# A first phase in chunks of 512 tokens instead of 384, on a kernel that runs on one TensorE

## The chip, the cores and the metric

The kernel runs on one core of one Trainium2 chip. The metric is the device time of one execution, in microseconds; lower is better. Engine names: PE (TensorE), DVE (VectorE), ACT (ScalarE), POOL (GpSimd), SP (the queue that issues most DMAs).

## The reference, cut to what matters

Linear attention, then a dense two-layer network, then a network of eight experts of which each token goes to one:

```
kv   = einsum('bhsd,bhse->bhde', k, v)            # 8 batches, 8 heads, 576 tokens, 64 wide
out  = einsum('bhsd,bhde->bhse', q, kv)
out  = out / sqrt(mean(out*out) + 1e-6) * g_norm  # per head
x    = out as [4608 tokens, 512]
h    = x @ w_in                                   # 512 -> 2048
y    = (max(h,0) + alpha*min(h,0)) @ w_out        # 2048 -> 512
e    = argmax(y @ w_gate + bias[modality]), p = softmax value of e
res  = p * (max(y @ w1[e], 0) @ w2[e])            # 8 experts, 512 -> 1024 -> 512
```

## The kernel before, in words

Every product of the networks is made of three products of a high part and a low part (hi x hi, hi x lo, lo x hi), all in fp32r.

The first phase takes the tokens in 12 chunks of CT = 384 (three tiles of 128). A chunk has 16 blocks `s`, one for each 128 of the 2048 hidden values. In block `s`, `first(c, s)` does 12 matmuls with the weights standing and the chunk's columns moving (L382, into a PSUM bank 384 wide). DVE then makes `gg` of it in two instructions (L388, L389), ACT rounds it to `ghi` (L393), POOL subtracts to `glo` (L395). `second(c, s - 1)` does nine matmuls (L409): each of ghi x w, ghi x w_low, glo x w for three tiles, 512 columns of the weights moving. So what `first(c, s)` gives is used one block later. At the chunk's end the next chunk's input is taken (`take_x`, L369, L370), and the last `second` is split over the boundary.

Between the matmuls each engine works, in program order, through what was put into the same blocks:

- `dots(c - 1)`: the eight routing logits of each tile of the chunk before, one DVE multiply-and-sum over 512 each (L426). DOTS says which of the 24 are done in which block; in the last chunk LAST_DOTS. Then `choose`, `weigh`, `count` (two small matmuls, L480, L481), `place`, `scatter` (indirect DMAs on POOL to the expert's rows in `xb`).
- For the next chunk: `kv_mm` (k times v of a batch that begins in it, 40 matmuls, L232), `attend` (q times kv, 64 matmuls for each tile, L249), `attended` (ACT copies and squares, L259, L260), `squares` (DVE sums, L295), `rsqrt`, `scale_x`, `turn_x`.
- Pieces of the expert weights: 128 times ACT rounds (L215) and POOL subtracts (L219) 512 columns, and SP stores them (`wsp`).

In chunk 0 the first network's weights come in and are cut into parts as they are used (`cut`), and before it there is a head: batch 0's kv, attention, norm and transposes for chunk 0, with idle transposes (`warm`, L858) on PE in between.

The second phase does 41 tiles of sorted rows, 24 matmuls a layer (`layer1`, `layer2`, L685). The first four tiles belong to one expert, chosen before the last chunk is routed; while they run, the last chunk's logits, places, `padding`, `table` and row loads are done. The order written there is the order on every engine's queue.

Of the kernel before, what the change touches and what calls it, by code (L numbers as in the profile page):

```python
# [26 lines left out]
CT = 384  # L27
# [16 lines left out]
DOTS = (0, 2, 5, 8, 11, 14, 17, 20, 22, 24)  # L44
LAST_DOTS = (0, 3, 7, 10, 14, 17, 21, 24)
# [3 lines left out]
def fused(ctx: ExitStack, tc, qT, kv, kv0, g2, wmoe, alpha, wgate, bias, modality, w12, out):  # L49
# [16 lines left out]
    kvt = phase1.enter_context(tc.tile_pool(name="kvp", bufs=1)).tile([128, 2, 5, 256], F32, name="kvt")  # L66
# [10 lines left out]
    pad = one.tile([128, ROW], F32, name="pad")  # L77
    yrow = [one.tile([128, ROW], F32, name=f"yrow{i}") for i in range(3)]
# [10 lines left out]
    xs = one.tile([128, 3, D], F32, name="xs")  # L89
# [17 lines left out]
    def other(n=512):  # L107
        return (pools[1] if pools else ps_a).tile([128, n], F32, tag="a", name="a")
# [117 lines left out]
    def kv_mm(b, p):  # L226
# [26 lines left out]
    def attended(c, t):  # L253
        ps = ops_t.pop((c, t))
        x = xs[:, t, :].rearrange("p (a h b) -> p a h b", a=4, h=2)
        sq = junk.rearrange("p (a h b) -> p a h b", a=4, h=2)
        xt_t[c, t] = xs[:, t, :].rearrange("p (a b) -> p a b", b=64)
        for h in range(2):
            A.copy(x[:, :, h, :], ps[h])  # L259
            A.activation(sq[:, :, h, :], ps[h], AF.Square)  # L260

    def kv_pair(p):

        t = kv_t.pop((0, p))
        kvp = ps_y.tile([128, 128], F32, tag="y", name="kvp") if p < 3 else bank(128)
# [9 lines left out]
    def attend_pair(p):  # L275
        for t in range(3):
            PE.matmul(ops[t][:, p, :], q_t[0][:, p, t * 128:(t + 1) * 128], kvbd[0][:, p, :], start=True, stop=True)

    def square_half(t, h):
        if t < 2:  # L280
            sq = (junk, pad)[t][:, h * 256:h * 256 + 256]
        else:
            sq = two.tile([128, CT], F32, tag="gg", name="sq")[:, 0:256]
# [7 lines left out]
    def squares(c, t):  # L291
        sq = junk.rearrange("p (a b) -> p a b", b=64)
        if t == 0:
            ms_t[c] = one.tile([128, 24], F32, tag="ms", name="ms")
        V.tensor_reduce(ms_t[c][:, t * 8:t * 8 + 8], sq, AX.X, ALU.add)  # L295

    def rsqrt(c, others=(), part=None):
# [5 lines left out]
        if c > 1:  # L303
            it, m = spare[:, 96:120].bitcast(I32), spare[:, 120:144]
        else:
            a = other(48) if c else bank(48)
            it, m = a[:, 0:24].bitcast(I32), a[:, 24:48]
        u = one.tile([128, 24], F32, tag="u", name="u")
# [6 lines left out]
        else:  # L315
            half, to = (one.tile([128, 24], F32, name=n) for n in ("half", "root"))
# [7 lines left out]
        if part == 0:  # L324
            sq = lambda: V.tensor_reduce(ms[:, 16:24], junk.rearrange("p (a b) -> p a b", b=64), AX.X, ALU.add)
            fill(list(others) + steps[:4], [sq])
        else:
            fill(steps, others)
# [15 lines left out]
    def scale_first(h):  # L344
        for t in range(3):
            r = ms_t[0][:, t * 8:t * 8 + 8]
            src = ops[t] if t < 2 else last
            to = xs[:, t, :].rearrange("p (h e a i) -> p a h e i", h=2, e=2, a=4)
# [4 lines left out]
    def turn_first(k):  # L353
        ps = ps_y.tile([128, CT], F32, tag="y", name="first") if k < 2 else spare[:, 0:CT] if k == 2 else bank(CT)
        for t in range(3):
            PE.transpose(ps[:, t * 128:(t + 1) * 128], xs[:, t, k * 128:(k + 1) * 128], ident)
        return ps

    def turn_x(c, t):
        x = xs[:, t, :]  # L360
        V.transpose(x, x)

    def take_x(c, k):
        if c:
            of = xs.rearrange("p t (a k j) -> p (t a) k j", a=4, k=4)[:, :, k]
# [7 lines left out]
    def first(c, fb, between=None):  # L373
# [9 lines left out]
        gg = two.tile([128, CT], F32, tag="gg", name="gg")  # L383
# [8 lines left out]
        ghi = two.tile([128, CT], F32R, tag="ghi", name="ghi")  # L392
        A.copy(ghi, gg)  # L393
        glo = two.tile([128, CT], F32R, tag="glo", name="glo")
# [3 lines left out]
    def second(c, fb, parts=(0, 1, 2)):  # L398
        ghi, glo = g_t[c, fb]
        if fb == 0:  # L400
            y_t[c] = [ps_y.tile([128, D], F32, tag="y", name="y") for _ in range(3)]
# [4 lines left out]
        for i in parts:  # L406
            a, w = steps[i]
            for t in range(3):
# [3 lines left out]
    B3 = [128, 3, E]  # L412
    ul = lambda a: a.unsqueeze(2).to_broadcast(B3)

    def y_out(c, t):
        if t == 1:
            lg_t[c] = one.tile([128, 3, E], F32, tag="lg", name="lg")
# [46 lines left out]
    def weigh(c):  # L464
# [3 lines left out]
        sm = one.tile([128, 3], F32, tag="sm", name="sm")  # L468
        V.tensor_reduce(sm, ex, AX.X, ALU.add)
        V.tensor_scalar(sm, sm, 1e-9, None, ALU.add)  # L470
        gate = one.tile([128, 3], F32, tag="gate", name="gate")
        V.reciprocal(gate, sm)
        for t in range(3):
            V.tensor_copy(yb_t[c][t][:, D:D + 1], gate[:, t:t + 1])
            V.tensor_copy(yb_t[c][t][:, D + 1:D + 2].bitcast(I32), tokid[:, c * 3 + t:c * 3 + t + 1])

    def count(c):
        hot, hb, lg = hot_t[c]
        ps = (other(48) if pools else spare[:, 0:48]).rearrange("p (n a b) -> p n a b", n=2, a=3)
# [4 lines left out]
    def place(c):  # L484
        hot, ps, _ = hot_t.pop(c)
        at = one.tile(B3, F32, tag="bt", name="at")
        for t in range(3):
# [3 lines left out]
        mx = one.tile([128, 3], F32, tag="mx", name="mx")  # L491
        V.tensor_reduce(mx, at, AX.X, ALU.add)
        pos = one.tile([128, 3], I32, tag="pos", name="pos")
# [12 lines left out]

    def padding():
# [4 lines left out]
        for e in range(E):  # L512
# [3 lines left out]
            i = SP.dma_start(xb[ds(r, 128)], pad)  # L516
# [22 lines left out]
    def table():  # L539
# [12 lines left out]
        tmp = two.tile([1, CT], F32, tag="gg", name="tmp")  # L552
# [17 lines left out]
        ge = two.tile([1, CT], F32, tag="gg", name="ge")[:, 0:NTAB * E].rearrange("p (a b) -> p a b", b=E)  # L570
# [60 lines left out]
    def load_rows(i):  # L631
# [7 lines left out]
        rows[i] = four(xs[:, i % 3, :])  # L639
# [6 lines left out]
    def load_first():  # L646
        r = SP.value_load(tab_0[0:1, 1:2], min_val=0, max_val=E * BUCKET)
        src = xb[ds(r, 3 * 128)]
        to = xs.rearrange("p t (a c) -> p (t a) c", a=4)
# [3 lines left out]
        for i in range(3):  # L653
            rows[i] = four(xs[:, i, :])
# [91 lines left out]
    def halves(i):  # L746
        if i not in ht:
            ht[i] = (pools[2].tile([128, 2, 512], F32R, tag="kv", name="hth"),
# [83 lines left out]
    with tc.manual_schedule():  # L832
# [28 lines left out]
        ops.extend(four(b) for b in (other(), other(), spare))  # L861
# [292 lines left out]
```

## Time and profile before

| | |
|---|---|
| median of 3 runs | 1342.45 us (1342.27 to 1343.2) |
| the profiled execution | 1342.6 us, span 1341.0 us |
| PE, DVE, POOL, ACT busy | 99%, 74%, 50%, 39% of the span |
| PEld (weight loads, beside PE) | 86% |
| first matmul of chunk 0 / first of the second phase | 20.34 us / 876.53 us |
| PE clock granted | 0.999 of full |

The span is from the first to the last instruction; the time adds what lies around it. "Busy" counts a matmul from its start to its modelled end, and matmuls overlap, so a PE that is busy all the time can still start its matmuls later than it might; the distance between starts tells that.

### The profile page before, as it was taken

How to read it: one execution, taken by the hardware profiler on the slowest of the kernel's cores; microseconds unless marked ns; L12 is line 12 of the kernel's file. 1: busy time of each engine (PE TensorE's matmuls, PEld its weight loads, DVE VectorE, ACT ScalarE, POOL GpSimd, SP SyncE). 2: the span in 40 equal slices, each digit the busy share in tenths (PEclk: the TensorE clock that was granted, in tenths of full speed). 3: DMA queues.
4: the chain of work that ended last, by engine and by line, in shares of the span. 5: the costliest groups of instructions: out<-in, count | busy, mean ns of one | idle time of the engine just before them, and what ended most of it. 6: DMA issues, size and time to landing. Idle time of an engine off the chain costs nothing. (4 is left out here: it accounts for less than half of the span.)

```text
span 1341.0 us, 26648 instructions
## 1 busy us (share of the span) xinstructions
PE 1332.3 (99%) x8864; PEld 1150.0 (86%) x8864; DVE 990.2 (74%) x2216; ACT 526.5 (39%) x1153; POOL 669.0 (50%) x648
## 2 busy tenths in 40 slices
PE   9999999999999999999999999999999999999997
PEld 8889888889888889888888988888888888888886
DVE  5789687878878777878687969576766666666664
ACT  5762323333333332332323331144544444444443
POOL 5867475656655555656474652353333333333321
PEclk9999999999999999999999999999999999999999
DMA  8955565554555564556564440547311271737784
GB/s 321 329 199 199 200 209 202 189 191 142 197 184 195 191 203 149 193 186 213 193 215 152 147 146 1 209 165 264 125 49 49 76 268 48 281 98 302 295 320 186
DMA packets 82325, 250.69 MB, mean 187 GB/s; under 512 B 12877, under 2 KB 32077, under 8 KB 80016
## 3 DMA queue, kind: packets, MB, share of 16 engines
q1 hardware_dynamic: 70432, 220.82, 46.3%
q0 software_dynamic: 11760, 28.14, 6.4%
q8 instruction: 78, 1.28, 0.4%
q14 instruction: 55, 0.45, 0.1%
HBM read 158.69 MB, written 91.54 MB: 187 GB/s over the span
## 5 line engine op out<-in xcount | busy, mean ns | idle before, releaser
L382 PE MATMUL h<-xhi,W 128*128 128x384 f32 x1536 | 427.7, 341 | 0.0
L395 POOL TENSOR_TENSOR glo<-gg,ghi 128x384 fp32r<-128x384 f32 x192 | 234.8, 1223 | 336.1 <-ACT ghi L393 330.4
L409 PE MATMUL y<-W,ghi 128*128 128x512 f32 x1152 | 298.7, 394 | 0.3 <-ACT ghi L393 0.2
L393 ACT CAST ghi<-gg 128x384 fp32r<-128x384 f32 x192 | 98.8, 515 | 502.0 <-DVE gg L389 249.3
L382 PEld LDWEIGHTS h<-xhi,W 128*128 128x128 f32 x1536 | 280.4, 188 | 9.4
L382 PE MATMUL h<-xlo,W 128*128 128x384 f32 x768 | 256.9, 337 | 0.0
L409 PEld LDWEIGHTS y<-W,ghi 128*128 128x128 f32 x1152 | 213.1, 188 | 39.4 <-ACT ghi L393 4.8
L426 DVE CUSTOM_DVE_ANT_0 junk<-yrow,wg_sb 128x512 f32<-128x512 f32 x242 | 220.3, 910 | 8.4 <-ACT yrow L420 2.8
L685 PE MATMUL h<-W,xhi 128*128 (+1 forms) x656 | 206.3, 395 | 0.0
L685 PE MATMUL y<-W,hth 128*128 (+1 forms) x656 | 204.4, 393 | 0.0
L219 POOL TENSOR_TENSOR raw<-raw 128x512 f32<-128x512 f32 x128 | 199.4, 1558 | 0.0
L388 DVE TENSOR_SCALAR gg<-h,alpha_sb 128x384 f32<-128x384 f32 x176 | 108.1, 614 | 107.8 <-PE h L382 107.4
L793 POOL DMA_INDIRECT out_dram<-kvbd,tail x41 | 43.4, 1059 | 279.6 <-ACT kvbd L791 238.7
L409 PE MATMUL y<-W,glo 128*128 128x512 f32 x576 | 163.8, 393 | 0.0
L382 PEld LDWEIGHTS h<-xlo,W 128*128 128x128 f32 x768 | 144.3, 188 | 6.0 <-DVE xlo L370 0.2
L685 PEld LDWEIGHTS h<-W,xhi 128*128 128x128 f32 x656 | 122.8, 187 | 29.9
L685 PEld LDWEIGHTS y<-W,hth 128*128 128x128 f32 x656 | 123.1, 188 | 26.6
L739 DVE TENSOR_SCALAR hh<-h 32x256 f32<-32x256 f32 (+1 forms) x320 | 129.0, 403 | 9.3 <-PE h L685 4.3
L685 PE MATMUL h<-W,xlo 128*128 (+1 forms) x328 | 129.3, 394 | 0.0
L409 PEld LDWEIGHTS y<-W,glo 128*128 128x128 f32 x576 | 107.6, 188 | 24.3 <-POOL glo L395 2.0
L685 PE MATMUL y<-W,htl 128*128 (+1 forms) x328 | 127.6, 389 | 0.0
L739 ACT ACTIVATE hh<-h 32x256 f32<-32x256 f32 (+1 forms) x320 | 117.4, 367 | 25.3 <-PE h L685 21.1
(216 smaller groups left out, 1402.7 us busy)
## 6 DMA issues: line engine op xcount, KB each, us to landing
wsp<-raw SPq DMA_DIRECT2D x128, 512.0 KB, 2.9
W<-wsp SPq DMA_DIRECT2D x16, 4096.0 KB, 14.1
raw<-in_w_dram SPq DMA_DIRECT2D x128, 256.0 KB, 3.3
kvt<-in_kv_dram SPq DMA_DIRECT2D x28, 512.0 KB, 7.0
xs<-xb POOLq DMA_DIRECT2D x140, 64.0 KB, 2.7
raw<-in_wmoe_dram SPq DMA_DIRECT2D x17, 511.8 KB, 6.0
qT<-in_qT_dram SPq DMA_DIRECT2D x11, 768.0 KB, 7.0
wg_sb<-in_wmoe_dram SPq DMA_DIRECT2D x15, 511.8 KB, 5.8
```

What stands on the lines that cost most here:

```text
L219: G.tensor_tensor(lo, lo, hi, ALU.subtract)
L382: PE.matmul(ps, w_at(fb, part)[:, k * 128:(k + 1) * 128], x[:, k, :], start=(i == 0), stop=(i == 11))
L388: V.tensor_scalar(gg, ps, 0.0, alpha_sb[:, fb:fb + 1], ALU.min, ALU.mult)
L393: A.copy(ghi, gg)
L395: G.tensor_tensor(glo, gg, ghi.bitcast(F32), ALU.subtract)
L409: PE.matmul(y_t[c][t], a[:, t * 128:(t + 1) * 128], w, start=(fb == i == 0), stop=(fb == NFB - 1 and i == 2))
L426: V.tensor_tensor_reduce(spare if i >= 22 else junk, y, wg_sb[:, e, :], 1.0, 0.0, ALU.mult, ALU.add, lg_t[c][:, t, e:e + 1])
L685: m = PE.matmul(ps, a, w, start=start, stop=stop)
L739: m = V.tensor_scalar(to, of, 0.0, None, ALU.max) if mine else A.activation(to, of, AF.Relu)
L793: d = G.indirect_dma_start(out=out, out_offset=IndirectOffsetOnAxis(ap=tail[:, i, 1:2].bitcast(I32), axis=0), in_=y, in_offset=None, bound ...
```

## The change

The first phase goes in nine chunks of 512 tokens, four tiles each. What comes with it: four PSUM banks for `y` and one less for attention and routing; `gg` has one buffer and not two; k and v share SBUF with the chunk's input, so they are loaded at the start of the chunk (first in SP's queue there) and not at the end of the one before; `attended` leaves its squares in PSUM, and DVE sums them from there behind the dots of the same block, in blocks 6 to 9 and not 9 to 11; `count` goes from block 9 to 11, `place` to 12; the pieces of expert weights go one to a block, 7 of them into the last chunk; chunk 0 cuts two weight halves in each block and never three; chunk 1's attention uses whole heads' pairs (16 matmuls a tile); the order of the second phase's start is new. Left out below are lines that only put NT (4) in the place of 3, or new names for the same memory.

```diff
-CT = 384
+CT = 512
+NT = CT // 128
-AT = 8
-AHEAD = (2, 4, 7)
-WARM = (14, 4, 0, 0, 0, 42)
+AT = 6
+AHEAD = ()
+WARM = (14, 4, 0, 0, 0, 46)
-FAR = [(1, e) for e in range(E)] + [(2, 6), (2, 7)]
+FAR = [(1, e) for e in range(E)] + [(2, e) for e in range(4, E)]
-DOTS = (0, 2, 5, 8, 11, 14, 17, 20, 22, 24)
-LAST_DOTS = (0, 3, 7, 10, 14, 17, 21, 24)
+DOTS = (0, 3, 7, 11, 15, 19, 23, 27, 30, 32)
+LAST_DOTS = (0, 4, 9, 14, 19, 24, 28, 32)
...
-    ps_y = ctx.enter_context(tc.tile_pool(name="ps_y", bufs=3, space=PSUM))
+    ps_y = ctx.enter_context(tc.tile_pool(name="ps_y", bufs=4, space=PSUM))
-    ps_a = phase1.enter_context(tc.tile_pool(name="ps_a", bufs=2, space=PSUM))
+    ps_a = phase1.enter_context(tc.tile_pool(name="ps_a", bufs=1, space=PSUM))
...
+    def pieces(c, s):
+        if c == NCH - 1:
+            return s < 7
+        return (1 + (s == 11) + (s == 4 and c < 3)) * (c > 0)
...
     def attend(c, ts):
+        if c == 1:
+            ps = four(other())
+            for a in range(4):
+                o = ts[0] * 128 + 32 * a
+                for p in range(4):
+                    PE.matmul(ps[32 * p:32 * p + 32, a, :], q[:, p, o:o + 32], kvbd[(c * CT + o) // S % 2][:, p, :], start=True, stop=True)
...
     def attended(c, t):
         for h in range(2):
             A.copy(x[:, :, h, :], ps[h])
-            A.activation(sq[:, :, h, :], ps[h], AF.Square)
+            A.activation(ps[h], ps[h], AF.Square)
...
     def squares(c, t):
-        V.tensor_reduce(ms_t[c][:, t * 8:t * 8 + 8], sq, AX.X, ALU.add)
+        for h, ps in enumerate(sq_t.pop((c, t))):
+            V.tensor_reduce(to[:, :, h], ps, AX.X, ALU.add)
...
-        gg = two.tile([128, CT], F32, tag="gg", name="gg")
+        gg = two.tile([128, CT], F32, tag="gg", name="gg", bufs=1)
...
+                if kvb and s == 0:
+                    load_kv(kvb[0], 0)
+                    load_kv(kvb[0], 1)
...
-                if 0 < c < NCH - 1 and (s < 12 or s == 14 and c <= 8):
+                for n in range(n_pre[0], n_pre[0] + pieces(c, s)):
...
-                if kvb and s in (3, 7):
+                if kvb and s in (2, 5):
...
+                    if nxt < NCH and AT <= s < AT + NT:
+                        squares(nxt, s - AT)
...
-                        if nxt < NCH:
-                            count(c - 1)
                         weigh(c - 1)
+                    if s == end + 3 and not last_one:
+                        count(c - 1)
...
-        dots(c, 16, 22)
+        dots(c, 16, 20)
         layer1(0, lambda: add(0, 1, 2))
         add(3)
         load_rows(3)
-        dots(c, 0, 5)
-        layer1(1, lambda: [add(4), turn_h(0), add(5, 6)])
-        dots(c, 5, 8)
-        add(7, 8, 9)
+        dots(c, 0, 7)
+        layer1(1, lambda: [add(4, 5), turn_h(0), add(6)])
+        dots(c, 7, 8)
+        dots(c, 24, 32)
+        add(*range(7, len(FAR)))
         choose(c)
         weigh(c)
+        clear(1)
         layer2(0)
-        count(c)
+        turn_h(1)
+        layer1(2, lambda: count(c))
         place(c)
-        turn_h(1)
-        scatter(c, range(3))
+        scatter(c, range(NT))
         padding()
         steps = table()
         next(steps)
         next(steps)
         load_rows(4)
         load_rows(5)
-        layer1(2)
         turn_rows(3)
```

## Rows read from the trace of the kernel before

**Rows 1.** Stretches of L382 alone: chunks 0, 6, 7, and chunk 11 without its last block.

```profile
20.33:93.93 73.60, 36.74 (x192) 33.58 (x193) 1.00 0.76 264
451.39:523.99 72.60, 36.62 (x192) 33.51 (x192) 1.00 0.53 180
523.99:593.54 69.55, 36.40 (x192) 33.64 (x192) 1.00 0.55 188
808.24:870.11 61.87, 33.93 (x180) 31.69 (x180) 1.00 0.29 102
```

**Rows 2.** Timeline of PE in chunk 5: start, length, line, count.

```profile
403.92 0.34 PE L382 MATMUL h<-xhi,W 128*128 128x384 f32 x1
...
406.01 1.54 PE L409 MATMUL y<-W,ghi 128*128 128x512 f32 x6
...
408.08 0.34 PE L382 MATMUL h<-xhi,W 128*128 128x384 f32 x1
```

**Rows 3.** The same where `attend` stands between two blocks.

```profile
417.24 0.85 PE L409 MATMUL y<-W,glo 128*128 128x512 f32 x3
...
419.43 0.44 PE L382 MATMUL h<-xhi,W 128*128 128x384 f32 x1
```

**Rows 4.** Stretches of L685 alone: one first and one second expert layer.

```profile
876.53:882.13 5.60, 5.60 (x24) 4.50 (x24) 1.00 0.37 158
888.61:894.11 5.50, 5.50 (x25) 4.32 (x23) 1.00 0.00 0
```

**Rows 5.** Timeline of DVE in chunk 6: one block, and `choose`.

```profile
461.20 0.61 DVE L388 TENSOR_SCALAR gg<-h,alpha_sb 128x384 f32<-128x384 f32 x1
...
463.04 0.69 DVE L426 CUSTOM_DVE_ANT_0 junk<-yrow,wg_sb 128x512 f32<-128x512 f32 x1
...
463.78 1.38 DVE L426 CUSTOM_DVE_ANT_0 junk<-yrow,wg_sb 128x512 f32<-128x512 f32 x1
...
465.09 0.61 DVE L388 TENSOR_SCALAR gg<-h,alpha_sb 128x384 f32<-128x384 f32 x1
...
492.27 1.08 DVE L450 TENSOR_TENSOR lg<-lg,bsel 128x24 f32<-128x24 f32 x1
```

**Rows 6.** Timeline of POOL in the same stretch.

```profile
463.10 1.51 POOL L395 TENSOR_TENSOR glo<-gg,ghi 128x384 fp32r<-128x384 f32 x1 [0.67 <-ACT ghi L393]
...
491.58 1.74 POOL L219 TENSOR_TENSOR raw<-raw 128x512 f32<-128x512 f32 x1
```

**Rows 7.** Groups by line: busy us, mean ns of one, idle before.

```profile
L389 DVE SCALAR_TENSOR_TENSOR gg<-h,gg 128x384 f32<-128x384 f32 x176 | 98.1, 557 | 6.0
...
L187 POOL TENSOR_TENSOR W<-yrow,W 128x512 fp32r<-128x512 f32 x32 | 41.2, 1297 | 7.7 <-ACT W L186 6.6
...
L764 DVE TENSOR_TENSOR htl<-turned,hth 128x512 fp32r<-128x512 f32 x6 | 3.8, 681 | 0.4 <-ACT hth L756 0.4
```

**Rows 8.** Timeline of all engines in the last chunk, around `first(11, 3)`.

```profile
819.38 0.34 PE L382 MATMUL h<-xhi,W 128*128 128x384 f32 x1
...
819.51 0.61 DVE L388 TENSOR_SCALAR gg<-h,alpha_sb 128x384 f32<-128x384 f32 x1
...
821.42 1.50 POOL L395 TENSOR_TENSOR glo<-gg,ghi 128x384 fp32r<-128x384 f32 x1 [3.12 <-ACT ghi L393]
...
822.98 0.96 PE L409 MATMUL y<-W,glo 128*128 128x512 f32 x3
```

**Rows 9.** The head: a stretch with all engines (us; PE, PEld, DVE, ACT, POOL busy; PEclk; DMA share; GB/s).

```profile
0.00:40.00 40.00, 38.20 (x270) 33.62 (x271) 25.43 (x60) 22.55 (x42) 23.83 (x46) 1.00 0.89 328
```

**Rows 10.** The head: timeline of all engines.

```profile
18.33 1.42 DVE L349 TENSOR_TENSOR xs<-a,root 128x256 f32<-128x256 f32 x4
```

**Rows 11.** Start of the second phase: timelines of PE and of DVE.

```profile
894.11 0.19 PE L480 MATMUL a<-hb,tri 128*128 128x24 bf16 x1
...
904.84 0.69 DVE L674 TENSOR_TENSOR xlo<-xs,xhi 128x512 fp32r<-128x512 f32 x1 [0.69 <-ACT xhi L672]
...
907.04 0.63 PE L685 MATMUL h<-W,xhi 128*128 128x512 f32 x2
```

More of the change, by code (lines that the diff above doesn't have):

```diff
@@ L76, in fused @@
     g_sb = one.tile([128, 4], F32, name="g_sb")
-    pad = one.tile([128, ROW], F32, name="pad")
-    yrow = [one.tile([128, ROW], F32, name=f"yrow{i}") for i in range(3)]
+    yrow = [one.tile([128, ROW], F32, name=f"yrow{i}") for i in range(4)]
     tri = one.tile([128, 128], BF16, name="tri")
@@ L88, in fused @@
     kvbd = [one.tile([128, 4, 128], F32, name=f"kvbd{i}") for i in range(2)]
-    xs = one.tile([128, 3, D], F32, name="xs")
+    kx = one.tile([128, 2560], F32, name="kx")
+    xs = [kx[:, t * D:t * D + D] for t in range(NT)]
+    xr = kx[:, 0:3 * D].rearrange("p (t c) -> p t c", c=D)
     xhi = one.tile([128, 4, CT], F32R, name="xhi")
@@ L315, in rsqrt @@
         else:
-            half, to = (one.tile([128, 24], F32, name=n) for n in ("half", "root"))
+            half, to = (one.tile([128, 8 * NT], F32, tag=n, name=m) for n, m in (("ex", "half"), ("bt", "root")))
             G.tensor_scalar(half, ms, -1.0 / 128, -0.5e-6, ALU.mult, ALU.add)
@@ L391, in first @@
             between()
-        ghi = two.tile([128, CT], F32R, tag="ghi", name="ghi")
+        g2 = two.tile([128, 2, CT], F32R, tag="g2", name="g2")
+        ghi, glo = g2[:, 0], g2[:, 1]
         A.copy(ghi, gg)
-        glo = two.tile([128, CT], F32R, tag="glo", name="glo")
         G.tensor_tensor(glo, gg, ghi.bitcast(F32), ALU.subtract)
@@ L400, in second @@
         if fb == 0:
-            y_t[c] = [ps_y.tile([128, D], F32, tag="y", name="y") for _ in range(3)]
+            y_t[c] = [ps_y.tile([128, D], F32, tag="y", name="y") for _ in range(NT)]
         whi, wlo = w_at(fb, 1), w_at(fb, 3)
@@ L860, in fused @@
         warm(WARM[0])
-        ops.extend(four(b) for b in (other(), other(), spare))
-        ms_t[0] = one.tile([128, 24], F32, tag="ms", name="ms")
+        ops.extend(four(b) for b in (other(), spare, *(ps_y.tile([128, 512], F32, tag="y", name="ops") for _ in range(2))))
+        ms_t[0] = one.tile([128, 8 * NT], F32, tag="ms", name="ms")
         for p in range(5):
@@ L883, in fused @@
         high_bits(0)
-        for t in range(3):
+        for t in range(NT):
             sum_half(t, 1)
@@ L943, in fused @@
                     SP.dma_start(bias_sb.rearrange("p a b -> p (a b)"), bias.rearrange("a b -> (a b)").partition_broadcast(128))
+                if c == 0 and s == 13:
+                    clear(0)
+                    for j in range(8):
+                        SP.dma_start(xb[E * BUCKET + j * 128:E * BUCKET + (j + 1) * 128], pad(0))
                 if edge and c == 0:
@@ L1027, in fused @@
-                    if nxt < NCH and end + 2 <= s < end + 5:
-                        scatter(c - 1, [s - end - 2])
-                    if nxt == NCH and s == 9:
+                        scatter(c - 1, range(NT) if last_one else (0, 1))
+                    if s == end + 5 and not last_one:
+                        scatter(c - 1, (2, 3))
+                    if last_one and s == 9:
                         load_first()
```

235 lines of the change are left out of this document (111 added, 124 removed).

## The prediction

> **What bounds the kernel now.** I read three views, in this order. The stretches by chunk: PE is on a matmul all the time, and chunks without a batch of k and v take the same time, so PE's own program is the bound and its length can be added up [rows 1]. The timeline of PE: a block takes 4.16 us, 2.09 for the 12 matmuls 384 wide (0.174 each) and 2.07 for the nine 512 wide (0.230 each) [rows 2]; the second phase starts its matmuls every 0.229 to 0.233 us, without a gap [rows 4]. The timelines of DVE and POOL: how far these two are from holding PE up. They are near it: where DVE had four dots in a block of the last chunk, `glo` came late and PE waited [rows 8]. The sum is made against the profiled execution: 1342.6 us, its span of 1341.0 and 1.6 around it; the median of the runs is 1342.45, the same within 0.02%. About 0.2%, 2.7 us, can be told from no change.
>
> **The matmuls of the blocks.** 192 blocks of 4.16 us are 798.7. After, 144 blocks have 12 matmuls 512 wide in `first` and 12 in `second`. `second` is 12 x 0.230 = 2.76. No row shows L382 at 512 columns. Its own 0.174 grows by the 53 to 55 ns that 128 more columns take (128 cycles at the granted 2.4 GHz level; or 0.229 less 0.174): 0.227 to 0.229. The highest row at 512 columns is 0.233 [rows 4]. I take 0.228, nearest to the line itself: `first` 2.74, block 5.50, 144 x 5.50 = 792.0, with rounding a gain of 7. At 0.233 the block is 5.56 and 1.5 us are lost; at 0.227, a gain of 8.
>
> The Trainium skill (TensorE: Matmul & The Clock Gate, "Wait — 56ns, not 53.3ns?") has matmuls of N columns follow each other at N/2.4 ns and 2.5 ns more. By it 576 matmuls fewer would save 576 x 2.5 ns = 1.4 us and no more. The rows do not bear it out for these fp32r matmuls: at 384 columns there are 14 ns beside the columns, and the sum goes by the rows.
>
> **What stands between the blocks.** A chunk without k and v would be 2.79 + 14 x 4.16 + 5.55 = 66.6 (at the boundary three matmuls of `second` change sides); it takes 69.55 [rows 1], so 2.97 is for two `attend` visits, `count` and a wait at the boundary. A visit of two tiles costs 2.19 - 0.69 = 1.50 [rows 3], and about 0.1 in the matmul behind it; the visit of one tile, `count` and the wait share the other 1.4. 11 chunks: 32.7. After: seven chunks with two visits of two tiles and a count, 3.3 each, and chunk 0 with four visits of 16 matmuls each, which stream as many columns as a tile's 64 did; bounded by 0.5 and 1.4 a visit, taken as 1.05 (the visit of one tile), 4.2. Together 27.3 (25 to 29), if the wait at the boundary goes: it is for `ghi` of block 15, which now has 2.76 us of `second` as cover, not 2.07. Gain 5.4. k and v: seven batches at 72.60 - 69.55 = 3.05 before and after.
>
> **Chunk 0.** 73.60 less 65.9, 3.05 and 2.97 leaves 1.7 us of waits for weights being cut. The cutting per block is the same work (two halves) in 5.50 us instead of 4.16, so most goes: I leave 0.6, gain 1.1. Bounds: gain 1.7, loss 2, if k and v ahead of the weights in SP's queue (1.2 MB, 3.6 us at 328 GB/s [rows 9]) make a half late; the halves are asked for three blocks ahead.
>
> **The head.** 0.26 MB more of q at 328 GB/s is 0.8; one tile more to sum 0.4; two scalings more, one of them before the first transposes, 1.42 / 4 = 0.36 [rows 10]; a transpose and wider takes 0.25. Chunk 0 begins 1.8 later, at 22.1. The four idle transposes more only fill this.
>
> **DVE and POOL.** This is the term against the change. A dot that meets a POOL subtraction waits for its end: 0.69 becomes 1.38 [rows 5], and ends 0.55 after it (465.16 after 464.61 [rows 6]). A subtraction that is asked for in the middle of a dot waits too: 1.74 where 512 columns take 1.30 alone [rows 6, 7]. The first step of `choose`, asked for during that one (491.58 to 493.32), takes 1.08 for 24 columns and ends with it [rows 5, 6]. So the two take turns, and who waits is next. Before, a block with three dots takes DVE 3.89 [rows 5], inside 4.16. After: 128 columns more are 0.12 to 0.13 each for L388 and L389 (0.557 to 0.681 [rows 7]), and a subtraction of 512 columns is 1.30 [rows 7]. Walk a block from L388's start, each step as in rows 5 and 6 with these columns added: the second dot from 2.1 (463.04 is 1.84 after 461.20); `glo` is asked for at 2.3, gets its turn at 2.75 when that dot ends, and ends at 4.04; the third dot, asked for at 2.85, ends at 4.56; the weight piece takes the turn until 5.76; the fourth dot ends at 6.3, and the next block's L388 starts at 6.2. With five dots 7.0. PE's block is 5.50. Before, the piece fell under L388 and L389, which it did not hold up.
>
> How late may DVE be? In rows 8 `glo` ended 3.4 us after L388's start, PE's next matmul came 0.06 after it, and L388 had started 2.2 us after `first`'s end; on time it starts 0.26 after. After the change `glo` is due 2.76 + 2.74 + 8 x 0.230 = 7.34 after `first`'s end, so L388 may be 7.34 - 4.04 - 0.06 - 0.26 = 2.9 us late.
>
> - Last chunk: L388 of block 0 to that of block 7 is 6.2 + 4 x 7.0 + 2 x 6.2 = 46.6 for DVE (4, 5, 5, 5, 5, 4, 4 dots, a piece in each), 3.66 + 6 x 5.50 = 36.7 for PE: 9.9 - 2.9 = 7.0 of waits. Before it waited 61.87 - (2.79 + 14 x 4.16) = 0.8. Loss 6.2. Without the fourth dot's wait it would be about 0.6, no loss.
> - Chunks 1 to 7: late by 0.9 at block 1 and 0.73 more at each block of four dots. In chunks 1 to 6 the k and v products give 1.5 back at blocks 2 and 5, and `attend` 1.6 at 6 and 8; the sums behind the dots wait for ACT's squares of the same block and add 0.9. It stays about 2.9: 0.15 of waits in each, 0.9 in all. Chunk 7 has no products: 1.5.
>
> `count` behind the root moves `place` to block 12 and the last scatter to 13; the rows scattered are overwritten in block 0 of the next chunk, two blocks (11 us) later, so that costs nothing; if the scatters took longer, ACT's copies of `y` would stand still there, and PE one block on. k and v first in SP's queue wait until the chunk's input is taken, with the stores and loads of weight pieces behind them: the first two parts (four DMAs) are due 14 us into the chunk and, at 1.2 MB and the head's rate, land in 8 to 11; late ones would hold PE itself, at the end of block 2. The other two parts go out behind the products of block 2 and are due three blocks later. The eight pad stores, moved from chunk 0's end to its block 13, go out after the last weights. One `gg` buffer holds nothing up: `glo` is done 4.04 after L388, before the next L388 at 5.5 or later.
>
> **Start of the second phase.** `count` stands in the middle of `layer1(2)`, 3.6 us further on in PE's program; `place` follows, two small sums longer, but the low half of tile 1 (1.3) is now ahead of it. So xlo of tile 3, done at 905.5 for a use at 907.04 [rows 11], is done 3.0 later, and PE waits about 1.25; between 0 and 3, as the 20 dots of DVE (14 before) fall.
>
> **Sum.** 7.2 + 5.4 + 1.1 gained; 1.8 + 6.2 + 1.5 + 0.9 + 1.25 lost: 2.05 us faster, 1340.5.
>
> **Rivals.**
> - *DVE keeps up* (other order of turns, or the pieces hide in L388 and L389 as before): no waits in the last chunk, chunk 7 or 1 to 6: 1340.5 - 8.5 = 1332. For it: average DVE work per block is within PE's time. Against: `choose` waited out a whole piece [rows 5, 6].
> - *Slower: DVE sets the block in every chunk.* It decides if lateness passes 2.9 in chunks 1 to 6 too, that is if the walk is 0.3 us short in a block, for one thing because the sums wait for ACT. Then three blocks more in each of six chunks cost 0.73: 13 us, 1353.
> - *Wider matmuls save little*: L382 takes the mean of rows 4, 0.231: block 5.53, 796.3, and the time is 1345 (1347 at 0.233). The skill's rule above comes to about the same. For it: three lines of this trace show 0.229 to 0.233 at 512 columns.
>
> **How the numbers follow.** The sum holds: 0.50 (own range 1337 to 1344; 0.20 of it faster, 0.28 same, 0.02 slower). DVE keeps up: 0.22, faster. DVE sets every chunk: 0.14, slower. Wider matmuls save little: 0.14, half same, half slower. Faster 0.42, same 0.35, slower 0.23. The range takes in DVE keeping up and the wide matmuls, and most of the slower case: 1332 to 1350.
>
> **What would show it.** L382 at 0.228 and blocks of 5.50 in chunk 7; first matmul of chunk 0 at 22.1; blocks 1 to 6 of the last chunk at 6.2 to 7.0 with PE's `second` waiting for `glo`; fourth dots of 1.8 us; the second phase beginning about 4 us earlier than 876.5, with one wait of 1 to 1.5 us before the fourth `layer1`. Last chunk's blocks at 5.5 would prove the walk wrong, blocks of 6 and more in chunks 1 to 6 would mean that the slack was misjudged.

## The result, and the profile after

The changed kernel takes 1350.7 us (median of six runs, 1349.47 to 1351.18) against 1342.4 for the kernel before beside it: a ratio of 1.006, with a 95% interval of 1.0047 to 1.0073. It is slower by 8 us, where 2 us faster was forecast, and it lies 0.7 us above the range. The profiled execution took 1350.9, its span 1349.3, the granted clock was 0.999.

In the new line numbers L397 is the first layer's matmul (L382 before), L424 the second layer's (L409), L403 and L404 make `gg` on DVE (L388, L389), L409 is ACT's high half, L410 POOL's `glo` (L395), L441 a dot (L426), L226 POOL's half of a weight piece (L219), L707 the second phase's matmul (L685). New here: L315 sums the squares on DVE, L495 is `count` on PE, L972 the eight zero writes (the prediction's pad stores), L1056 the load of the gate weights.

Stretches of L397 alone, as in [rows 1]: chunks 0, 1, 4 and 7, and the last chunk without its last block.

```profile
22.72:118.41 95.69, 47.84 (x193) 35.67 (x193) 1.00 0.64 201
118.41:217.06 98.65, 47.79 (x193) 35.67 (x193) 1.00 0.59 206
408.25:503.53 95.28, 47.78 (x193) 35.67 (x193) 1.00 0.55 188
694.56:787.53 92.97, 47.58 (x193) 35.82 (x192) 1.00 0.45 156
787.53:875.59 88.06, 44.42 (x181) 33.72 (x180) 1.00 0.47 171
```

Chunk 4 stands for the quiet ones: chunks 3, 4 and 6 take the same 95.28. Chunk 0 begins at 22.72 (20.33 before [rows 1]). Chunk 1 takes 3.4 more than chunk 4; chunks 2 and 5, not shown, took 95.91 and 95.75, 1.1 more together. The last chunk's PE program without waits is 3.71 (block 0: 12 matmuls of `first`, four of `second`) + 14 x 5.54 = 81.3, so it waited 6.8.

The 5.54 comes from PE's timeline, here one block of chunk 7, as in [rows 2].

```profile
698.27 0.39 PE L397 MATMUL h<-xhi,W 128*128 128x512 f32 x1
...
701.05 2.91 PE L424 MATMUL y<-W,g 128*128 128x512 f32 x12
...
703.80 0.40 PE L397 MATMUL h<-xhi,W 128*128 128x512 f32 x1
```

The 12 matmuls of `first` take 701.05 - 698.27 = 2.78, 0.232 each (0.174 at 384 columns [rows 2]), the 12 of `second` 2.75, 0.229 each. A block is 5.53 here, 5.54 on the mean: 144 of them are 797.8, and the 192 before were 798.7.

The timeline of all engines in one five-dot block of the last chunk answers to [rows 5, 6, 8].

```profile
803.62 0.75 DVE L403 TENSOR_SCALAR gg<-h,alpha_sb 128x512 f32<-128x512 f32 x1
...
805.87 3.04 PE L424 MATMUL y<-W,g 128*128 128x512 f32 x12 [0.60 <-ACT g L409]
805.90 1.68 POOL L410 TENSOR_TENSOR g<-gg,g 128x512 fp32r<-128x512 f32 x1 [3.49 <-ACT g L409]
...
806.47 1.66 DVE L441 CUSTOM_DVE_ANT_0 junk<-yrow,wg_sb 128x512 f32<-128x512 f32 x1
807.54 1.74 POOL L226 TENSOR_TENSOR raw<-raw 128x512 f32<-128x512 f32 x1
...
808.17 1.66 DVE L441 CUSTOM_DVE_ANT_0 junk<-yrow,wg_sb 128x512 f32<-128x512 f32 x1
...
810.49 0.75 DVE L403 TENSOR_SCALAR gg<-h,alpha_sb 128x512 f32<-128x512 f32 x1
```

The third dot and the fourth take 1.66 each: one meets `glo`, the other the weight piece. From L403 to the next L403 are 6.87 us, longer than PE's 5.54, and PE waits. It waits for ACT's `ghi` (0.60 us here); over the last chunk the trace puts 4.3 us of PE's idle time to `ghi` and 0.3 to POOL's `glo`, which both follow from the same late L403.

DVE at the head of chunk 1, and the loads that SP had issued before it (two timelines).

```profile
122.27 0.69 DVE L404 SCALAR_TENSOR_TENSOR gg<-h,gg 128x512 f32<-128x512 f32 x1
127.41 0.69 DVE L441 CUSTOM_DVE_ANT_0 junk<-yrow,wg_sb 128x512 f32<-128x512 f32 x1 [4.46 <-DMA wg_sb<-in_wgate_dram]
```

```profile
109.42 4.81 SPq L972 DMA_DIRECT2D xb<-yrow  x8
114.34 1.00 SPq L219 DMA_DIRECT2D raw<-in_w_dram  x2
115.40 0.50 SPq L1056 DMA_DIRECT2D wg_sb<-in_wgate_dram  x1
120.07 0.38 SPq L130 DMA_DIRECT2D kx<-in_kv_dram  x1
```

The first dot waits 4.46 us for the gate weights `wg_sb`. Their 2 MB are issued behind eight zero writes of 257 KB each, another 2 MB, which stood behind them before. SP itself stood for 12.6 us in front of the first zero write, until POOL had cleared the row that it writes (done at 109.39), and the gate weights, which come after these writes in its program, went out only then.

The second phase, PE's timeline where tile 3's first layer begins, answers to the last of [rows 11].

```profile
914.18 0.40 PE L707 MATMUL y<-W,htl 128*128 128x512 f32 x1
914.99 0.73 PE L707 MATMUL h<-W,xhi 128*128 128x512 f32 x2 [0.42 <-ACT xhi L694]
915.72 0.50 PE L707 MATMUL h<-W,xlo 128*128 128x512 f32 x1
```

From the second phase's first matmul (883.88) to the one at 914.99 are 31.11 us, against 907.04 - 876.53 = 30.51 before [rows 4, 11]. That start comes 0.81 after the one ahead of it, where 0.23 is usual: PE waits for `xhi` first. By the start at 916.06, three matmuls on, it is another 0.4 behind; in between stands the wait for `xlo`.

### The profile page after: what moved, and what is told of

Same layout as the page of the kernel before. It is cut to its first block, busy times and chain, and to the rows that moved or that the text cites. A ratio compares the mean times of both kernels' runs of the same rounds, so it can differ in the third digit from the quotient of the medians.

```text
span 1349.3 us, 24692 instructions
## 1 busy us (share of the span) xinstructions
PE 1331.8 (99%) x8106; PEld 1075.5 (80%) x8106; DVE 992.8 (74%) x2062; ACT 519.8 (39%) x1092; POOL 648.9 (48%) x604
## 4 chain that ended last, share of the span: by engine, by line
issue 37%; PE 34%; POOL 11%; DVE 9%; DMA 5%; POOLq 2%; SPq 1%; ACT 1%; DVEq 0%; ACTq 0%
PE h L397 16%; PE y L424 14%; POOL raw L226 5%; DVE junk L441 4%; POOL g L410 3%; DMA raw<-in_w_dram 2%; DVE gg L403 1%; DVE gg L404 1%; POOL kx L664 1%; PE h L707 1%; DMA wsp<-raw 1%; POOL out_dram L815 1%; DMA out_dram<-kvbd,tail 1%; POOLq L660 1%; PE a L239 1%
## 5 line engine op out<-in xcount | busy, mean ns | idle before, releaser
L424 PE MATMUL y<-W,g 128*128 128x512 f32 x1728 | 420.9, 392 | 6.1 <-ACT g L409 5.7
L424 PEld LDWEIGHTS y<-W,g 128*128 128x128 f32 x1728 | 323.5, 188 | 82.5 <-ACT g L409 10.9
L397 PE MATMUL h<-xhi,W 128*128 128x512 f32 x1152 | 387.1, 398 | 0.0
L410 POOL TENSOR_TENSOR g<-gg,g 128x512 fp32r<-128x512 f32 x144 | 214.3, 1488 | 353.7 <-ACT g L409 314.8
L441 DVE CUSTOM_DVE_ANT_0 junk<-yrow,wg_sb 128x512 f32<-128x512 f32 x256 | 277.1, 1082 | 11.1 <-DMA wg_sb<-in_wgate_dram 4.5
L409 ACT CAST g<-gg 128x512 fp32r<-128x512 f32 x144 | 89.4, 621 | 497.9 <-DVE gg L404 439.9
L397 PEld LDWEIGHTS h<-xhi,W 128*128 128x128 f32 x1152 | 216.2, 188 | 52.2 <-issue 0.8
L397 PE MATMUL h<-xlo,W 128*128 128x512 f32 x576 | 226.0, 395 | 0.2 <-issue 0.2
L707 PE MATMUL h<-W,xhi 128*128 (+1 forms) x656 | 206.4, 396 | 0.4 <-ACT xhi L694 0.4
L707 PE MATMUL y<-W,hth 128*128 (+1 forms) x656 | 204.5, 393 | 0.0
L226 POOL TENSOR_TENSOR raw<-raw 128x512 f32<-128x512 f32 x128 | 196.7, 1539 | 9.3 <-ACT raw L222 9.2
L403 DVE TENSOR_SCALAR gg<-h,alpha_sb 128x512 f32<-128x512 f32 x128 | 95.3, 745 | 99.6 <-PE h L397 88.6
L707 PEld LDWEIGHTS h<-W,xhi 128*128 128x128 f32 x656 | 122.7, 187 | 30.5 <-ACT xhi L694 0.8
L707 PEld LDWEIGHTS y<-W,hth 128*128 128x128 f32 x656 | 123.2, 188 | 26.5
L707 PE MATMUL h<-W,xlo 128*128 (+1 forms) x328 | 129.4, 394 | 0.0
L397 PEld LDWEIGHTS h<-xlo,W 128*128 128x128 f32 x576 | 108.2, 188 | 25.0 <-issue 0.5
L707 PE MATMUL y<-W,htl 128*128 (+1 forms) x328 | 127.6, 389 | 0.0
L404 DVE SCALAR_TENSOR_TENSOR gg<-h,gg 128x512 f32<-128x512 f32 x128 | 88.5, 691 | 4.4
```

Source lines behind the costliest of these rows:

```text
L226: G.tensor_tensor(lo, lo, hi, ALU.subtract)
L397: PE.matmul(ps, w_at(fb, part)[:, k * 128:(k + 1) * 128], x[:, k, :], start=(i == 0), stop=(i == 11))
L403: V.tensor_scalar(gg, ps, 0.0, alpha_sb[:, fb:fb + 1], ALU.min, ALU.mult)
L404: V.scalar_tensor_tensor(gg, ps, 0.0, gg, ALU.max, ALU.add)
L410: G.tensor_tensor(glo, gg, ghi.bitcast(F32), ALU.subtract)
L424: PE.matmul(y_t[c][t], a[:, t * 128:(t + 1) * 128], w, start=(fb == i == 0), stop=(fb == NFB - 1 and i == 2))
```

## Experiments

Edits are to the changed kernel unless another is named. Chunk totals are read as above, from the first matmul of L397 in one chunk to that of the next.

### What a wider matmul costs

```
-  PE.matmul(ps, w_at(fb, part)[:, ...], x[:, k, :], ...)
+  n = WIDTH.get(c, CT) if i else CT      # by chunk
+  PE.matmul(ps[:, 0:n], w_at(fb, part)[:, ...], x[:, k, 0:n], ...)
```

> Eleven of the twelve matmuls of the first layer's line move fewer columns in chunks 2 to 8: 448, 384, 320, 256, 192, 128 and 480; chunk 1 keeps 512. The rest of each product is left out, so only the time from one matmul to the next inside a run of twelve is read. Theory (time goes by columns alone, 0.452 ns each, as 0.174 at 384 columns before and 0.232 at 512 after say): 0.217 us at 480, 0.203 at 448, 0.174 at 384, 0.145 at 320, 0.116 at 256, 0.087 at 192, 0.058 at 128. Rival 1, the forecast's (a fixed part of about 0.012 us in each matmul, 0.174 at 384 and 0.228 at 512): 0.201 at 448, 0.147 at 320, 0.120 at 256, 0.066 at 128, and 512 columns slowed to 0.232 by something else in this kernel. Rival 2 (the changed kernel slows every matmul by 2%, whatever its width): 384 columns take 0.177 or more here.

Stretches of this line alone, each from the second of a block's twelve matmuls to the first of `second`, so eleven matmuls of one width: 512, 480, 448, 384, 320, 256, 192 and 128 columns. The granted clock is 1.00 in all, the 2.4 GHz level. The run's own time (1378.86, one run) is not read: PE stands waiting in the narrow chunks, and its granted clock fell to 0.985 on the mean.

```profile
199.02:201.58 2.56, 2.56 (x12) 1.88 (x10) 1.00 0.89 317
776.79:779.20 2.41, 2.41 (x12) 1.87 (x10) 1.00 0.00 0
220.88:223.12 2.24, 2.24 (x12) 1.88 (x10) 1.00 0.94 258
315.15:317.08 1.93, 1.93 (x12) 1.76 (x10) 1.00 0.93 275
407.55:409.16 1.61, 1.61 (x12) 1.51 (x10) 1.00 0.86 227
503.99:505.29 1.30, 1.30 (x12) 1.25 (x10) 1.00 0.53 188
597.94:599.14 1.20, 1.20 (x12) 1.19 (x10) 1.00 0.47 163
690.29:691.47 1.18, 1.18 (x12) 1.17 (x10) 1.00 0.24 97
```

Divided by eleven: 0.233, 0.219, 0.204, 0.175, 0.146, 0.118, 0.109, 0.107. Down to 256 columns that is 0.454 to 0.462 ns a column. Between 256 and 512 one more column costs (2.56 - 1.30) / 11 / 256 = 0.447 ns, which leaves 4 ns in each matmul that do not go with the columns: the theory had none, rival 1 had 12. The theory is within 0.002 from 512 to 320 columns. Rival 1 fits at 320, misses by 0.003 at 448, and has 0.054 for the step from 384 to 512, which is 0.058 here; at 256 the two are off alike, by 0.002. Rival 2 fails at 384. Below 256 both fail: there is a floor near 0.108, and no price per column. Four matmuls of 384 columns cost what three of 512 cost (0.70), and 576 matmuls fewer save 1 to 2 us.

### Whose turn it is in the last chunk

```
  e2   last chunk: -  return s < 7              +  return 0
       others:     -  (s == 11) + (s == 4 and c < 3)   +  (s in (11, 14)) + (s == 4 and c < 3)
  e5   last chunk: -  return s < 7              +  return s < 2
       others:     -  (s == 11) + (s == 4 and c < 3)   +  (s in (4, 11))
  e12  in the kernel before:
       -  if 0 < c < NCH - 1 and (s < 12 or s == 14 and c <= 8):
       +  if c > 0 and (s < (7 if c == NCH - 1 else 12) or s == 14 and c == 1):
```

> The seven pieces of the last chunk move to the fifteenth block of chunks 1 to 7; the last chunk's dots stay. Theory (in the last chunk VectorE and GpSimd take turns, and the pieces are what fills GpSimd's half): its blocks 2 to 8 fall from 6.1 to 6.9 us to about 5.6, its waits from 6.8 to under 1, chunks 1 to 7 lose at most 0.5 together, the time is 1344 to 1345.5. Rival (the dots themselves are too many for a block, or are slow since they read PSUM): the blocks stay above 6.1, the time is 1349 or more.

Measured 1348.01, ratio 1.0038 (1.0025 to 1.0051). The stretches of its chunk 1 and of its last chunk, and one five-dot block there on DVE:

```profile
117.98:217.94 99.96, 47.78 (x192) 35.66 (x192) 1.00 0.60 204
...
791.70:873.75 82.05, 44.67 (x180) 33.61 (x180) 1.00 0.33 122
```

```profile
806.42 0.74 DVE L403 TENSOR_SCALAR gg<-h,alpha_sb 128x512 f32<-128x512 f32 x1
...
809.27 1.66 DVE L441 CUSTOM_DVE_ANT_0 junk<-yrow,wg_sb 128x512 f32<-128x512 f32 x1
...
810.97 0.69 DVE L441 CUSTOM_DVE_ANT_0 junk<-yrow,wg_sb 128x512 f32<-128x512 f32 x1
...
812.32 0.75 DVE L403 TENSOR_SCALAR gg<-h,alpha_sb 128x512 f32<-128x512 f32 x1
```

In the last chunk the theory holds: 88.06 falls to 82.05, the fourth dot is back at 0.69, a block of five dots takes DVE 5.90, and PE no longer waits for it. The total missed its mark, since chunks 1, 2 and 4 to 7 lost some 4.6 us, most of it to the second piece in their fifteenth block, which came before its weights had landed and held up ACT.

> Five of the last chunk's seven pieces go to the fifth block of chunks 3 to 7, where chunks 1 and 2 have a second piece already and lose nothing by it; two stay in the last chunk's blocks 0 and 1. Theory (the turns of VectorE and GpSimd cost the last chunk 6 us; a second piece costs nothing where its weights have landed, and ScalarE waited for them in the fifteenth block of the run before): last chunk 82 to 82.6, chunks 3 to 7 as in the changed kernel within 0.3, the time 1344.3 to 1345.5. Rival (any second piece in a block of chunks 3 to 7 makes ScalarE wait): chunks 3 to 7 each lose 0.3 to 1, the time 1346.5 to 1348.

Measured 1346.92, ratio 1.003 (1.0019 to 1.0042). Chunks 3, 4, 6 and 7 are as in the changed kernel, so a second piece in the fifth block costs nothing; but the last chunk took 83.4, 2.0 more than the 81.45 of the run with all repairs, so the two pieces left in it still cost that. In this profile chunk 1 lost 1.1 more at its head, where PE stood 2.3 us for ACT's `ghi` and the granted clock was 0.50 for the 3.4 us behind it, and chunk 5 lost 1.2 more.

> One part of the change alone, in the kernel before: seven of its 128 pieces go to the last chunk's blocks 0 to 6 (taken from the fifteenth blocks of chunks 2 to 8), at 384 tokens a chunk and with three or four dots a block. Theory (VectorE and GpSimd take turns, and what a block costs is the sum of both engines' work in the turns): a block of four dots goes from 4.6 to about 5.6 us, one of three from 4.2 to about 4.9, the last chunk is 5 to 9 us longer, the time 1347 to 1351. Rival (the last chunk of the changed kernel is slow only since it has five dots a block there): the last chunk at most 2 us longer, the time 1344 or less.

Measured 1346.14, ratio 1.0026 (1.0015 to 1.0036): one part of the change alone costs the kernel before 3.4 us. The last chunk without its last block, 61.87 in [rows 1]:

```profile
807.82:873.61 65.79, 33.95 (x180) 31.72 (x180) 1.00 0.49 172
```

3.9 us more, between the two marks. PE's blocks 2, 3, 5 and 7 lengthened by 0.8 to 1.2, the others not. On DVE four blocks paid 0.98 each, the three with four dots and block 0 with three: the last dot there took 1.66, since it met the piece. In blocks 2, 4 and 6, with three dots, the piece fell under the two operations for `gg` and cost nothing (L388 to the next L388 stays 3.90 us with a piece, as 3.89 in [rows 5]). The turns are real, but their price depends on what stands next to them.

### What stands ahead of the gate weights

```
  e3   if c == 0 and s == 13:  +  SP.dma_start(wg_sb, ...)   ahead of clear(0) and the eight zero writes
       edge of chunk 0:        -  SP.dma_start(wg_sb, ...)
  e4   -  if kvb and s == 0:   +  if kvb and s == (c == 1):
  e9   as e3, and clear(0) in block 8, the zero writes in block 12 of chunk 0 (so ahead of the gate weights again)
```

> The load of the gate weights is issued at the end of chunk 0's fourteenth block, ahead of the eight zero writes, not behind them. Theory (2 MB of zero writes moved ahead of the gate weights in SP's queue, and chunk 1's first dot waits 4.46 us for them): that wait is gone, chunk 1 falls from 98.65 to 95.5 to 96.3 us, and the time by 2.4 to 3.2, to 1347.5 to 1348.5. Rival (the k and v loads at chunk 1's head share the engines, and whatever is last there comes late): chunk 1 stays within 0.7 of 98.65, since the zero writes now delay k and v, or ScalarE waits for the zero writes before it may refill their row.

Measured 1348.4, ratio 1.0043 (1.0027 to 1.006), chunk 1 at 95.97: the theory, with 0.7 of the rival, since ACT now waited 1.44 before it refilled the zero row (the trace names a load of k and v there, but by the program it is the zero writes that hold that row).

> In chunk 1 alone the first two k and v loads are issued one block later. Theory (the zero writes ahead of the gate weights make them late): the wait of chunk 1's first dot keeps 3.5 us or more, and k and v, later, hold PE up as well; time 1350 to 1352. Rival (k and v beside the gate weights make them late): the first dot waits under 2 us, chunk 1 falls to 97 or less, time 1349 or less.

Measured 1350.54, ratio 1.0058 (1.0041 to 1.0075), chunk 1 at 98.51. The first dot on DVE's timeline waited as long as ever; k and v are not the cause.

```profile
127.55 0.69 DVE L441 CUSTOM_DVE_ANT_0 junk<-yrow,wg_sb 128x512 f32<-128x512 f32 x1 [4.35 <-DMA wg_sb<-in_wgate_dram]
```

> The eight zero writes are issued one block earlier, in chunk 0's block 12, their row cleared in block 8, and the gate weights behind them in block 13, so that neither waits for a cleared row and both have landed before chunk 1's first activation. Theory (the order of these two in SP's queue is the whole of chunk 1's extra 3.4 us; what was left with the gate weights ahead was ScalarE waiting for the zero writes): chunk 1 95.2 to 95.6 us, no wait of a first dot over 0.5, the time 1347 to 1348. Rival (the k and v loads beside the first two pieces keep a part of it): chunk 1 stays at 96 or more, the time at 1348.4 or more.

Measured 1347.45, ratio 1.0038 (1.0025 to 1.0051). SP's timeline, and chunk 1's stretch:

```profile
96.38 6.06 SPq L972 DMA_DIRECT2D xb<-yrow  x8
106.41 0.34 SPq L974 DMA_DIRECT2D wg_sb<-in_wgate_dram  x1
```

```profile
117.98:213.25 95.27, 47.77 (x192) 35.66 (x192) 1.00 0.55 188
```

Chunk 1 takes 95.27, the quiet chunks' time. The zero writes stand ahead of the gate weights here too, but nothing waits for their row, and the gate weights go out at 106.41 instead of 115.40. So it was not the order as such: the late issue of the gate weights, behind the wait for the row and behind the writes, was the whole of chunk 1's extra 3.4 us.

### The second phase

```
  layer1(2, lambda: count(c))
+ turn_rows(3)
  place(c)
  ...
- turn_rows(3)
```

> In the second phase the turning of row tile 3 goes ahead of the last places and the table, on all engines. Theory (its low half comes late and costs layer 1 of tile 3 the gap of 0.81 us that the changed kernel shows): the gap is gone, the second phase's first six tiles' halves take 36.0 to 36.5 and not 37.1 us, the time falls by 0.5 to 1. Rival (the table is what the second phase waits for next): the row loads and the expert's weights come 1.4 us later, a gap opens further on, the time stays within 0.4.

Measured 1353.17, ratio 1.0075 (1.0058 to 1.0092), 2.5 slower. Tile 3's first layer now comes on time, 30.54 after the first matmul, and a gap opens further on, as the rival has it; but it is another wait than the rival's, and a dearer one: DVE reaches the later halves `htl` late, and PE waits 1.41 and 1.01 for them.

```profile
922.30 0.51 PE L707 MATMUL y<-W,htl 128*128 128x512 f32 x1 [1.41 <-DVE htl L786]
929.11 0.50 PE L707 MATMUL y<-W,htl 128*128 128x512 f32 x1 [1.01 <-DVE htl L788]
```

### The two moves that were priced at little

```
  e7   if s == end + 1:       +  count(c - 1)          ahead of weigh
       if s == end + 3:       -  count(c - 1)
  e8   +  squares(nxt, s - AT)      ahead of dots
       dots(c - 1, at[s], at[s + 1])
       -  squares(nxt, s - AT)
```

> In chunks 1 to 7 the count goes back to directly behind the choice, two blocks earlier than in the changed kernel, ahead of the root. Theory (its place is worth nothing: TensorE's two small matmuls cost 0.1 to 0.2 us wherever they stand, and VectorE has room in both blocks): the chunk totals move by less than 0.3 each, the time by less than 1. Rival (TensorE waits for the choice's last step where the count stands right behind it): 0.3 to 1 us per chunk, 2 to 7 in all.

Measured 1377.23, ratio 1.0257 (1.024 to 1.0275): 26.5 us slower than the changed kernel, and the theory is wrong. PE's row for `count` in chunk 3, and the sum on DVE that it waited for:

```profile
385.60 0.19 PE L495 MATMUL spare<-hb,tri 128*128 128x32 bf16 x1 [2.15 <-DVE ms L315]
```

```profile
385.13 0.42 DVE L315 TENSOR_REDUCE ms<-spare 128x4 f32<-128x256 f32 x1 [0.15 <-ACT spare L274]
```

`count` writes to the bank `spare`. The squares now lie there too, until DVE has summed them. In this place `count` meets the sum of the fourth tile's squares and must wait for it, and PE's program waits with it: 18.6 us in seven waits. Behind five of them (2.15 to 3.48 us) PE's granted clock is down, behind the other two (1.70 and 2.13) it is not. A stretch of PE's next matmuls in chunk 3 (all engines' columns first, then L397 alone):

```profile
383.00:385.60 2.60, 0.45 (x2) 0.12 (x2) 0.90 (x3) 2.23 (x7) 2.07 (x2) 1.00 0.08 29
```

```profile
386.23:388.79 2.56, 2.56 (x8) 1.98 (x6) 0.50 0.74 232
```

Having stood for 2.15 us, PE goes at a granted clock of 0.50, the 1.2 GHz level, and a matmul takes 0.427 instead of 0.232. Some 36 matmuls in all do so, 7 us; with the waits and the slow first matmuls behind them that is the 26. The rival was nearer, but it named another wait, the choice's last step, and a fourth of the price. So it is the squares in `spare` that ask for the later `count`; `count` early in another bank was not tried.

> In chunks 1 to 7 the sums of squares stand ahead of their block's dots, not behind them. Theory (VectorE then waits for ScalarE's squares with four dots queued behind it, and the dots push the next block's activation): blocks 6 to 9 lengthen by 0.3 to 1 us each, 1 to 3 per chunk, the time by 7 to 20. Rival (ScalarE is done in time, and blocks 6 to 9 have room on VectorE): chunk totals within 0.3, the time within 1.

Measured 1370.61, ratio 1.0206 (1.0189 to 1.0223), 20 us slower, the upper end of the theory. DVE's timeline in chunk 3:

```profile
377.58 0.42 DVE L315 TENSOR_REDUCE ms<-a 128x4 f32<-128x256 f32 x1 [1.83 <-ACT a L274]
...
378.50 1.15 DVE L441 CUSTOM_DVE_ANT_0 junk<-yrow,wg_sb 128x512 f32<-128x512 f32 x1
```

DVE stands still for 1.83 us with the dots behind it, and the first dot then meets a POOL subtraction.

### The repairs together

```
  e10  the issues of e9, and
       pieces:   last chunk 0;  others 1 + (s in (4, 11)) + (c == NCH - 2 and s in (1, 9))
       layer1(1, lambda: [add(4, 5), turn_blocks(3), turn_h(0), add(6)])
       add(*range(7, len(FAR))); take_rows(3, 0)
       -  turn_rows(3)     +  take_rows(3, 1)
  e11  as e10, with s in (1, 8) in chunk 7
```

> All three repairs: the zero writes and gate weights as in the run beside it; no piece in the last chunk, a second one in the fifth block of chunks 3 to 7 and in blocks 1 and 9 of chunk 7; and row tile 3's transposition on VectorE in the gap in which it waits for ScalarE's half of tile 0, its high half on ScalarE ahead of the choice, its low half where it was. Theory, summed: 1350.7 less 3.2 (chunk 1), 6.0 (last chunk at 82 to 82.3), 0.6 to 0.9 (the gap of 0.81 in the second phase) is 1340.6 to 1340.9; with a part of it eaten by new waits 1341 to 1342. Rival (the waits are handed on: chunk 7 with 20 pieces turns slow, as the last chunk did): chunk 7 96 or more, the time 1343.5 or more, slower than the kernel before.

Measured 1342.97 (11 runs), ratio 1.0003 (0.9993 to 1.0012). Stretches of chunks 1, 7 and the last, and tile 3's first layer in PE's timeline:

```profile
118.68:213.97 95.29, 47.79 (x193) 35.67 (x193) 1.00 0.55 188
692.54:787.52 94.98, 47.56 (x193) 35.81 (x193) 1.00 0.51 175
787.52:868.97 81.45, 44.38 (x181) 33.73 (x181) 1.00 0.32 120
```

```profile
907.79 0.63 PE L707 MATMUL h<-W,xhi 128*128 128x512 f32 x2
```

Chunk 1 and the last chunk are without waits, and tile 3 starts 30.54 after the second phase's first matmul (877.25). Chunk 7 paid 2.0 for its 20 pieces, and the time is that of the kernel before.

> The three repairs again, with chunk 7's two further pieces in blocks 1 and 8, not 1 and 9. Theory (in the run before, chunk 7's twelfth block took 8.09 us, 2.0 more than in the changed kernel, since the third piece buffer had not come round: a doubled block needs two single ones ahead of it): chunk 7 back to 92.9 to 93.4 us, the time 1341 to 1341.8, at or a little below the kernel before's 1342.5. Rival (any two more pieces in chunk 7 cost it 2 us, wherever they stand): chunk 7 94.5 or more, the time 1342.6 or more.

Measured 1343.98 (11 runs), ratio 1.0008 (0.9999 to 1.0017). Chunk 7 took 95.88: the rival; two more pieces cost it 2 to 3 us in either place. Neither version beats the kernel before.

## Why the prediction was wrong

Against the kernel before, profiled execution against profiled execution (1342.6 and 1350.9), in us:

| term | forecast | measured |
| --- | --- | --- |
| start of chunk 0 | +1.8 | +2.4 |
| the matmuls of the blocks | -7.2 | -0.9 |
| chunk 1 beyond a quiet chunk | 0 | +3.4 |
| chunks 2 and 5 beyond a quiet chunk | 0 | +1.1 |
| waits in the last chunk | +6.2 | +6.0 |
| second phase | +1.25 | +1.0 |
| the rest: between blocks, chunk 0, small waits | -4.1 | -4.7 (what is left) |
| sum | -2.05 | +8.3 |

**The step that failed is the price of L382 at 512 columns.** The prediction took 0.174 and the 53 to 55 ns "that 128 more columns take", 0.228, and held 14 ns beside the columns to be fixed. The line takes 0.232; the step from 384 to 512 is 0.058, one third of the 0.174. The 14 ns were what is left of 0.174 if a column costs one cycle of 2.4 GHz, a price that no row showed; the widths put it at 0.447 ns, so 10 of the 14 ns went with the columns and only about 4 are fixed. That is 6.3 of the 10.4 us, and the rival "wider matmuls save little" had it right at 0.231. The one number of the trace that bore on the slope at this very line was 0.174 / 384 = 0.453 ns; times 512 it gives 0.232.

The Trainium skill's rule that the prediction weighed (TensorE: Matmul & The Clock Gate, "Wait — 56ns, not 53.3ns?"; N/2.4 ns and 2.5 more) would put 512 columns at 215.8 ns and 256 at 109.2, estimates from that page: the rows, 0.233 and 0.118 us, are 8% longer at both. The form, a price per column and a few ns, is there, with 0.447 ns a column in place of 1/2.4 = 0.417; and its consequence, hardly a saving, came true. The floor near 0.108 is close to 107 ns, an estimate for loading 128 weight columns by the Trainium skill's P/1.2 ns (same page, "LDWEIGHTS (loading the stationary operand)"). In the trace a load's row lasts 0.19 us at 128 and at 512 columns alike and overlaps the next; that the load is what sets the floor was not tried.

**A transfer was priced alone.** The eight pad stores, in the prediction, "go out after the last weights"; it did not ask what goes out after them. The gate weights did, behind SP's wait for the cleared row and the writes themselves, and chunk 1's first dot waited: 3.4 us, shown by the run that issues the gate weights 9 us sooner. With the matmuls this is nearly all of the miss. k and v, named as the risk, landed in time: a later issue changed nothing.

**Right, and shown.** The turns of VectorE and GpSimd: 6.87 and 6.14 per block of five and of four dots, where 7.0 and 6.2 were walked out, the third and fourth dot at 1.66, waits of 6.8 against 7.0; taking the pieces out gave back 6.0. What PE waited for was mostly `ghi`, not `glo` as forecast; the two fall due so close together (in the block shown `glo` is done at 807.58, and PE comes to it at about 807.7) that the sum did not feel it. The boundary's wait for `ghi` went: from the last block's first matmul to the next chunk's are 7.37 in quiet chunks, 5.54 and eight matmuls of 0.229. The second phase's wait at tile 3 was there, for `xhi` and then for `xlo`, 1.0 in all against 1.25.

**Off by a little.** Chunk 0 began 2.4 later, not 1.8; in the runs that leave the head alone it began anywhere from 22.23 to 23.20, so this is within its scatter. The 2.4 us that chunks 1 to 7 were to lose to late DVE were not there: PE's trace shows no wait in chunks 3, 4 and 6 and one of 0.3 in chunk 7; the sum hides this, since the rest of that row, the time between blocks and chunk 0, came out dearer. The extra 0.5 us in chunk 5 are a stop of PE in its tenth block (below); of chunk 2's 0.6, 0.3 is a wait of `count` for DVE (L358), and the rest was not traced. Two figures beside the sum are off: at 0.227 the matmuls would gain 9 us, not 8, and the rival's 0.233 would make 1349 (1340.5 with the gain of 7.2 gone and 1.5 lost), not 1347.

**Priced without their reason.** `count` and the sums of squares were costed in their new places only, and the prediction does not say why they moved. Each would have cost 20 us or more in the other place: the two moves gain nothing by themselves, but with the squares left in PSUM they save that. That the forecast came out right here owes nothing to its working.

## What to carry to other kernels

A matmul that streams several hundred columns may have hardly any fixed price: before betting on fewer, wider ones, divide the row's spacing by its columns and multiply. When a transfer is moved ahead in a queue, price the transfers that it now stands ahead of, look up who reads them first, and what it will itself wait for there. Two engines that take turns are full long before their busy shares add up to a chunk; walk one block in turns, and put the second engine's work where the first has none.

## What was not expected of the hardware

- These fp32r matmuls follow each other at 0.454 to 0.462 ns a column from 256 to 512 columns, at a granted clock of 1.00, which is 1.09 to 1.11 cycles of 2.4 GHz (0.447 ns for each further column and about 4 ns besides); and at 0.107 to 0.109 us for 128 and for 192 columns alike. At a granted clock of 0.50 the same 512 columns took 0.427, which is 512 / 1.2 GHz and nothing more.
- In nine of the twelve profiles with nine chunks PE stopped between the first and the second matmul of chunk 5's tenth block, there alone, for 0.1 to 1.6 us. In the run with all repairs this row is "1.28 <-issue": the profile shows nothing that it waited for. The DMA packets of these traces point at the loading of instructions. In all nine a 16 KB packet of the instruction queue q8 (72 of them in the changed kernel's run) ends near the first matmul (0.97 us ahead of it to 0.46 behind), and PE goes on 1.28 to 1.52 us after that end. In two of the other three the packet ended 0.92 and 1.49 us ahead of the first matmul, in the third none lay there. Other packets of q8 lie beside matmuls that do not stop, and no run moved this one, so that PE waits for its instructions is likely and not shown.
- A piece cost DVE 0.98 us in blocks where the last dot met it, and nothing where it fell under the two operations for `gg` (the kernel before, with pieces in its last chunk): what a turn costs depends on who asks next.
